# Forming both signs of a head pair's kv sum in one pass over the values, in a linear-attention block on one core

## The chip, the cores and the metric

The kernel runs on one core of a Trainium2 chip. The metric is the device time of one execution in microseconds. "Span" is the length of one profiled execution, which lies about 2 us under the timed value. Engines are called by the profile's names: PE (TensorE matmuls), PEld (its weight loads), DVE (VectorE), ACT (ScalarE), POOL (GpSimd).

## The reference

```python
# S = 2048 tokens, D = 448, H = 16 heads of Dh = 28, F = 1792
def A(x, wqkv, w_phi, wo):                       # linear attention
    q, k, v = split_heads(x @ wqkv)
    pq, pk = q @ w_phi, k @ w_phi                # per head
    phi_q = concat(softmax(pq), softmax(-pq))    # 56 features: two signs of 28
    phi_k = concat(softmax(pk), softmax(-pk))
    kv, z = sum_s phi_k[s] v[s]^T, sum_s phi_k[s]
    o = (phi_q @ kv) / (phi_q @ z + 1e-6)
    return merge_heads(o) @ wo
h   = x + A(layernorm(x), ...)
out = h + (sigmoid(g) * u) @ w_down              # g, u = layernorm(h) @ w_gate, w_up
```

The sums over tokens are a barrier: the first `num` product (`phi_q @ kv`, called num0) needs the kv sum of all 16 token blocks.

## The kernel before

Each engine works through a hand-made list of named operations (`ORDER`); semaphores between the lists come from the reads and writes that each operation declares. TensorE runs with its array split into two halves of 64 rows, LO and HI, whose matmuls are interleaved. The code keeps the two halves from writing one PSUM bank at the same time: an operation that puts the *other* half on a bank first waits for the previous one to be done with it. The code calls this crossing. A projection of one token block is two such operations, `pva` then `pvb`, on the same two banks with the halves exchanged; the list puts other work between them.

For each block t: ScalarE makes exp(+) and exp(-) of the projected keys (`ek`), VectorE sums them per head and sign (`ss`) and inverts (`rs`), POOL or VectorE multiplies (`phi`), and PE adds phi^T v into banks 6 and 7 (`kva`, `kvb`).

```python
NX, NO, NH, NPHI, NS, NE, NV, NSG, NHH = 3, 4, 3, 3, 3, 5, 5, 4, 2   # ring depths: NPHI phi slots, NV value slots
...
def kvf(first):                       # one kv op: 4 matmuls on LO, 4 on HI
    def f(e):
        def part(half, sg):           # weights: one sign of FOUR heads (120 columns); stream: their 4 x 29 values
            vv = v1[half, sv, :, :].rearrange("p (a h) e -> p a h e", a=2)
            return [(bk(6 + sg)[:GR, gg*4*EV:(gg+1)*4*EV], phi[half, sp, sg, gg, 0:GR],
                     vv[:, :, 2*gg:2*gg+2, :], ...) for gg in range(G)]
        sg = int(first != (t % 2 == 0))
        return both(e, part(LO, sg), part(HI, 1 - sg))
...
def kvmask():                         # keep each head's own block, 2 ops of 464 columns on VectorE
    for sg in (1, 0):
        op("dve", "kvz%d" % sg, lambda e, sg=sg: e.tensor_tensor(kvz[:, sg, ...], bk(6 + sg)[:GR, 0:G*4*EV]...,
           maskK[:]..., ALU.mult), r=[B(6 + sg), "maskK"], w=["kvz%d" % sg])
```

The softmax here doesn't subtract the row's maximum and nothing guards it: scores larger than these inputs give would overflow.

Of the kernel before, what the change touches and what calls it, by code (L numbers as in the profile page):

```python
# [6 lines left out]
ALU = mybir.AluOpType  # L7
# [11 lines left out]
class Graph:  # L19
# [86 lines left out]
    def emit(self, nc):  # L106
# [71 lines left out]
P = 128  # L178
D = 448
# [19 lines left out]

QL, QH = slice(0, 56), slice(64, GR)  # L200
# [3 lines left out]
        "x1 x0 ld_k0 x2 ld_k2 x4 x6 ld_v0 x10 ld_v2 ld_q2 x8 ld_q3 ld_q1 ld_q0 xT4 xT5 xT6 x14 x12 xT7 ld_woe1 xT8 "  # L204
        "xT9 xT10 xT11 xT12 xT13 xT14 ld_woo1 xT15 ld_wd0 ld_woe0 ld_wu2 ld_wg0 ld_wg2 ld_wd1 ld_wg3 ld_wu3 ld_woo0 "
        "ld_wu0 ld_wg1 ld_wd4 ld_wd6 ld_wu1 oT3 oT2 oT4 oT5 oT6 oT7 hT2 ld_wd3 ld_wd2 hT3 ld_wd5 hT4 oT8 oT9 hT5 hT6 "
# [4 lines left out]
        "wphi3 wphi2 wphi1 wphi0 wTe1 wTe0 wTe3 w2e0_0 w2e0_1 w2e0_2 w2e0_3 xn3 xn4 ek0 ek1 xn5 v1_0 v1_1 xn6 ek2 ek3 "  # L211
        "v1_2 w2e1_1 v1_3 xn7 ek4 w2e1_3 xn9 w2e1_2 ek5 v1_5 v1_6 ek6 xn11 ek7 xn12 ek8 v1_8 xn13 ek9 xn14 ek10 v1_10 "
        "ek11 v1_11 ek12 v1_12 ek13 v1_13 ek14 eq0_0 ek15 v1_14 v1_15 eq0_1 eq1_0 eq1_1 eq2_0 oT0e eq2_1 sq0 sq1 "
        "eq3_0 eq3_1 sig0_1 sig0_0 sig0_3 sig0_2 sig0_5 sig0_4 sig0_7 sq2 sig0_6 sq3 sig0_9 sig0_8 sig0_10 sig0_11 "
        "sq5 sig0_12 sig0_13 sq4 sq7 sig2_0 sig2_1 sq6 sig2_3 sig2_2 sig2_5 sig2_4 sig2_6 sig2_7 sig2_8 sig2_9 "
        "sig2_10 sig2_11 sig2_12 sig2_13 sig4_1 sq9 sig4_0 sig4_3 sq8 sig4_2 sig4_5 sig4_4 sig4_7 sig4_6 sig4_9 sq10 "
        "sig4_8 sq11 sig4_11 sig4_10 sig4_13 sig4_12 sig8_1 sig8_0 sq13 sig8_2 sig8_3 sig8_4 sig8_5 sq12 sig8_6 sq14 "
        "sq15 sig8_7 sig8_9 sig8_8 sig8_10 sig8_11 sig8_13 sig8_12 sig12_0 sig12_1 sig12_3 sig12_2 sig12_5 sig12_4 "
        "sig12_7 sig12_6 sig12_8 sig12_9 sig12_11 sig12_10 sig12_12 sig12_13 "
    ),  # L220
    "pe": (
        "warm0 wT1 wT0 warm1 xT1 warm2 xT0 warm3 wT2 wT3 w2m0_0 warm4 w2m0_1 w2m0_3 w2m0_2 warm5 xT2 warm6 ppa0 warm7 "
        "ppb0 xT3 vva0 vvb0 ppa2 ppb2 vva2 vvb2 kva0 w2m1_1 w2m1_0 kvb0 kva1 pva4 kvb1 pvb4 w2m1_3 w2m1_2 pva5 pva6 "
        "pvb5 pvb6 kva2 pqa0_0 kvb2 pva7 kva3 pvb7 pva8 kvb3 pvb8 pva9 kva4 pvb9 kvb4 pva10 kva5 pvb10 pva11 kvb5 "
        "kva6 pvb11 kvb6 pva12 kva7 pvb12 pva13 kvb7 pvb13 kva8 pva14 kvb8 kva9 pvb14 kvb9 pqb0_0 kva10 pva15 kvb10 "
        "kva11 pvb15 kvb11 kva12 pqa0_1 kvb12 kva13 pqb0_1 kvb13 kva14 pqa1_0 kvb14 kva15 kvb15 pqb1_0 pqa1_1 num0 "
        "num1 pqb1_1 pqa2_0 pqb2_0 num2 pqa2_1 oT0 pqb2_1 oT1 num3 woa0 wob0 pqa3_0 num4 pqb3_0 pqa3_1 pqb3_1 num5 "
        "hT0 hT1 ga0_1 gb0_1 ga0_0 num6 gb0_0 ga0_3 woa2 gb0_3 ga0_2 wob2 gb0_2 num7 ga0_5 gb0_5 ga0_4 gb0_4 ga0_7 "
        "gb0_7 ga0_6 num8 gb0_6 woa4 ga0_9 ga0_8 gb0_9 gb0_8 wob4 ga0_11 ga0_10 gb0_11 gb0_10 woa6 num9 wob6 ga0_13 "
        "ga0_12 gb0_13 gb0_12 dn0_0 dn0_4 ga2_0 ga2_1 gb2_0 gb2_1 dn0_8 dn0_11 ga2_3 num10 ga2_2 gb2_3 dp0_0 gb2_2 "  # L230
        "dp0_4 ga2_5 ga2_4 gb2_5 gb2_4 dp0_8 dp0_11 ga2_6 ga2_7 gb2_6 gb2_7 woa8 ga2_8 ga2_9 gb2_8 gb2_9 wob8 num11 "
        "ga2_10 ga2_11 gb2_10 gb2_11 dn2_0 ga2_12 ga2_13 gb2_12 gb2_13 dn2_4 dn2_8 ga4_1 num12 gb4_1 ga4_0 dn2_11 "
        "gb4_0 dp2_0 ga4_3 ga4_2 gb4_3 dp2_4 num13 gb4_2 ga4_5 dp2_8 gb4_5 ga4_4 dp2_11 gb4_4 ga4_7 num14 gb4_7 ga4_6 "
        "woa10 gb4_6 ga4_9 wob10 gb4_9 ga4_8 num15 gb4_8 ga4_11 woa12 gb4_11 ga4_10 wob12 gb4_10 ga4_13 dn4_0 ga4_12 "
        "gb4_13 gb4_12 dn4_4 ga8_1 ga8_0 gb8_1 gb8_0 dn4_8 dn4_11 ga8_3 ga8_2 dp4_0 gb8_2 dp4_4 dp4_8 gb8_3 ga8_4 "
        "dp4_11 gb8_4 ga8_5 woa14 gb8_5 ga8_6 wob14 gb8_6 ga8_7 dn6_0 gb8_7 dn6_4 ga8_8 ga8_9 dn6_8 gb8_9 gb8_8 "
        "dn10_0 dn6_11 ga8_11 ga8_10 gb8_11 gb8_10 dp6_0 dp6_4 dp6_8 ga8_13 ga8_12 gb8_13 gb8_12 dp6_11 dn10_4 dn10_8 "
        "ga12_0 ga12_1 gb12_0 dn8_0 dn10_11 gb12_1 ga12_2 dp10_0 ga12_3 dn8_4 gb12_3 gb12_2 dp10_4 dn8_8 ga12_5 "
        "dn8_11 ga12_4 gb12_5 gb12_4 dp8_0 dp8_4 ga12_7 ga12_6 gb12_7 dp10_8 dp10_11 gb12_6 dp8_8 dp8_11 ga12_9 "
        "ga12_8 gb12_9 gb12_8 dm14_0 dm12_0 dm15_0 ga12_11 ga12_10 gb12_11 gb12_10 dm12_4 dm14_4 dm13_0 ga12_12 "  # L240
        "ga12_13 gb12_12 gb12_13 dm15_4 dm14_8 dm15_8 dm12_8 dm15_10 dm14_10 dm14_12 dm14_13 dm15_12 dm12_10 dm12_12 "
        "dm15_13 dm12_13 dm13_4 dm13_8 dm13_10 dm13_12 dm13_13 "
    ),
    "dve": (
        "zero bd0 bst1 agg1 bst0 agg0 ve1_0 nm1_0 nm1_1 xn1 bst2 bst3 agg2 agg3 ve1_3 xT0e wTe2 bst5 nm1_3 bst4 agg5 "
        "agg4 bst6 xT1e ve1_4 bst7 agg7 agg6 bst10 xT2e bst11 agg10 xT3e nm1_6 ss0 agg11 rs0 ss1 bst8 rs1 bst9 agg8 "
        "ss2 agg9 ss3 w2e1_0 rs3 rs2 v1_4 bst15 bst14 bst13 ss4 agg14 agg13 bst12 rs4 agg15 agg12 xn10 ss5 ss6 v1_7 "
        "rs6 rs5 ss7 rs7 ss8 v1_9 ss9 rs9 rs8 xn15 ss10 ss11 rs11 rs10 ss12 rs12 ss13 phi11 ss14 rs13 rs14 phi13 ss15 "
        "rs15 phi15 kvz1 kvz0 rsm0 qq0 rsm1 b0 c0 qq1 den0 b1 rden0 c1 rsm2 den1 qq2 rden1 b2 c2 den2 oT1e rsm3 rden2 "
        "qq3 b3 c3 h0 den3 nm0 rden3 h1 rsm4 nm1 qq4 b4 c4 den4 hn0 hn1 rsm5 hT0e hT1e qq5 b5 c5 den5 rden4 hh0_1 "  # L250
        "rsm6 qq6 rden5 b6 hh0_0 c6 den6 rden6 hh0_3 h2 rsm7 hh0_2 qq7 b7 hh0_5 c7 nm2 hh0_4 den7 rden7 h3 nm3 rsm8 "
        "hh0_7 hh0_6 hn2 qq8 b8 hn3 hh0_9 hh0_8 h5 h4 nm5 c8 nm4 den8 hh0_10 hh0_11 rsm9 qq9 h6 h7 b9 c9 hh0_12 "
        "hh0_13 nm7 rden8 nm6 den9 hh2_0 hh2_1 hn4 rsm10 rden9 qq10 b10 hh2_3 c10 hh2_2 hn6 hn7 den10 hh2_5 hh2_4 "
        "fin0 fin1 hh2_6 hh2_7 hn5 rden10 hh2_8 hh2_9 h8 h9 hh2_10 hh2_11 rsm11 qq11 nm9 b11 hh2_13 c11 hh2_12 den11 "
        "rsm12 qq12 nm8 b12 c12 rden11 hh4_1 hh4_0 o10 den12 hh4_3 rsm13 qq13 b13 rden12 hh4_2 c13 hh4_5 den13 fin3 "
        "hn9 rden13 hh4_4 hn8 fin2 rsm14 hh4_7 o13 qq14 b14 c14 hh4_6 den14 h10 h11 nm10 hh4_9 nm11 rsm15 hn10 hh4_8 "
        "hn11 hh4_11 qq15 h13 h12 hh4_10 b15 c15 hh4_13 nm13 hh4_12 den15 nm12 rden15 o15 rden14 hh8_1 hh8_0 o14 "
        "hh8_2 hh8_3 fin4 fin5 hh8_4 hh8_5 h15 h14 nm14 hh8_6 nm15 hn12 hn14 hh8_7 hh8_9 hh8_8 hn13 hn15 hh8_11 "
        "hh8_10 hh8_12 hh8_13 fin6 fin7 hh12_0 hh12_1 hh12_3 hh12_2 hh12_5 hh12_4 hh12_7 fin11 hh12_6 fin9 fin10 fin8 "
        "hh12_8 hh12_9 hh12_11 hh12_10 hh12_12 hh12_13 fin14 fin15 fin12 fin13 "  # L260
    ),
    "pool": (
        "ident0 phipad wqpad mask0 neghalf ident ve1_1 pow1_1 pow1_0 xn0 v1ones mask1 nm1_2 ve1_2 pow1_2 nb1_2 xn2 "
        "pow1_3 nm1_4 nb1_3 pow1_4 nb1_4 ve1_6 opad0 mask2 pow1_6 nb1_6 phi0 phi1 nm1_8 ve1_8 pow1_8 nb1_8 xn8 phi2 "
        "phi3 ve1_12 nm1_12 pow1_12 kvzones nb1_12 phi4 phi5 phi6 phi7 phi8 phi9 phi10 phi12 phi14 o0 o1 o2 o3 ve0 "
        "pow2_0 ve1 pow2_1 o4 o5 o6 o7 ve2 pow2_2 ve3 pow2_3 ve5 ve4 pow2_4 o8 pow2_5 ve7 o9 ve6 pow2_7 pow2_6 ve8 "
        "ve9 o11 pow2_9 o12 pow2_8 ve10 pow2_10 ve11 pow2_11 ve12 pow2_12 ve14 pow2_14 ve15 ve13 pow2_15 pow2_13 "
# [38 lines left out]
def build(nc, A_x, A_wqkv, A_w_phi, A_wo, B_w_gate, B_w_up, B_w_down, out):  # L306
# [10 lines left out]
    with ExitStack() as es:  # L317
# [6 lines left out]
        maskK = sb("maskK", [GR, 4, EV], f32)  # L324
# [26 lines left out]
        wu_sb = sb("wu_sb", [P, KT, F])  # L351
        wd_sb = sb("wd_sb", [P, FT, D])
        xnT = [sb("xnT%d" % c, [P, KT, 512]) for c in range(NCH)]
        hnT = xnT
        eq = [sb("eq%d" % c, [GR, 2, G, 512]) for c in range(NCH)]
        hhT = [sb("hhT%d" % c, [P, FT, 512]) for c in range(NHH)]
        ek = hhT[1][:].rearrange("p f n -> p (f n)")[:, 0:NE * 2 * D].rearrange("p (s a d) -> p s a d", s=NE, a=2)
        ss = sb("ss", [P, NE, 2 * H], f32)
        rs = sb("rs", [P, NE, 2 * H], f32)
        phi = sb("phi", [P, NPHI, 2, G, P])  # L360
        v1 = sb("v1", [P, NV, H, EV])
        kvz = sb("kvz", [GR, 2, G, 4 * E])
        rsm = sb("rsm", [P, NS, H], f32)
# [524 lines left out]
```

## Time and profile before

| | before |
|---|---|
| time, median of 3 | 208.84 us (208.36 to 208.96) |
| first kv op / num0 / first gate matmul start | 17.56 / 47.58 / 61.09 us |
| the stage between the first two, here "kv stage" | 30.02 us |
| all 32 kv ops, each from its start to the next operation's start | 7.54 us |

Busy sums of matmuls overlap, so what a kv op costs PE is read from the timeline as the distance between starts (sums of these are good to about 0.03 us). Two more are needed: the end of the kv stage on PE and on VectorE (columns: start, time, engine, line, operation, count).

```profile
45.13 1.10 PE L289 MATMUL psum<-v,phi 64*120 64x116 bf16 x24
46.07 1.68 PE L289 MATMUL psum<-xnT,Wq 64*120 64x512 bf16 x14
47.58 0.60 PE L289 MATMUL psum<-kvz,eq 56*128 56x60 bf16 x31
```
```profile
46.27 1.19 DVE L657 TENSOR_TENSOR kvz<-psum,maskK 120x464 bf16<-120x464 f32 x2 [1.01 <-PE psum L289]
```

While VectorE copies the finished sum through the mask, PE runs two halves of the query projection. Num0 starts right behind them: the copy is hidden.

### The profile page before, as it was taken

The page shows a single profiled execution, that of the slowest core. Times are in us where ns is not written, and L with a number is a line of the kernel's source. Part 1 is how long each engine was busy: PE and PEld are TensorE (multiplying, and loading weights), DVE is VectorE, ACT ScalarE, POOL GpSimd, SP SyncE. Part 2 cuts the span into 40 slices and gives each one's busy share as a digit, 9 for nine tenths or more (in the row PEclk, how much of TensorE's full clock was granted, in tenths as well). Part 3 has the DMA queues.
Part 4 walks back from the last instruction along what each step waited for, and adds up shares of the span by engine and source line. Part 5 has one row for each costly group of instructions (what it writes and reads, how often), then busy time and mean ns, then how long its engine had stood idle before and what let it go on. Part 6 is the DMA issues. An engine that isn't in the chain of part 4 may idle for free.

```text
span 206.8 us, 5794 instructions
## 1 busy us (share of the span) xinstructions
PE 199.2 (96%) x2457; PEld 112.6 (54%) x2457; DVE 136.6 (66%) x343; ACT 95.2 (46%) x185; POOL 59.0 (29%) x99
## 2 busy tenths in 40 slices
PE   7999999999989999999999999999999999999991
PEld 2935666775446666777444444444555555544450
DVE  4899999978899897767768967446332513353151
ACT  2689999878792536222333342324323122122100
POOL 4868999831345404400032020001400000000000
PEclk9999999999999999999999999999999999999997
DMA  5945344899122270413005411030321000020013
GB/s 156 292 107 135 82 95 88 247 382 258 56 51 54 44 166 32 79 25 55 3 0 91 109 29 25 15 41 22 78 49 25 3 0 3 0 89 3 0 37 119
DMA packets 32722, 16.25 MB, mean 79 GB/s; under 512 B 24952, under 2 KB 31800, under 8 KB 32696
## 3 DMA queue, kind: packets, MB, share of 16 engines
q1 hardware_dynamic: 32192, 15.86, 31.2%
q8 instruction: 19, 0.31, 0.6%
q10 hardware_dynamic: 504, 0.03, 0.2%
q14 instruction: 7, 0.06, 0.1%
HBM read 8.34 MB, written 1.84 MB: 49 GB/s over the span
## 4 chain that ended last, share of the span: by engine, by line
PE 86%; DVE 4%; POOL 3%; DMA 2%; issue 1%; ACT 1%; SPq 1%
PE psum L289 79%; PE psum L814 5%; DMA x_sb<-in_A_x_dram 2%; POOL o_pad L700 1%; PE psum L478 1%; POOL rst L728 1%; SPq L388 1%; DVE hn_pad L732 1%; DVE st L485 1%; ACT eq L637 0%; PE psum L553 0%; ACT eq L638 0%; POOL xn_pad L514 0%; PE psum L464 0%; DVE hhT L788 0%
## 5 line engine op out<-in xcount | busy, mean ns | idle before, releaser
L289 PE MATMUL psum<-xnT,wg_sb 64*128 64x512 bf16 (+1 forms) x490 | 94.6, 333 | 0.7 <-DVE qq L685 0.6
L289 PE MATMUL psum<-xnT,wu_sb 64*128 64x512 bf16 (+1 forms) x490 | 94.5, 334 | 0.3
L787 ACT ACTIVATE sg_sb<-psum 128x512 bf16<-128x512 f32 (+1 forms) x70 | 35.0, 512 | 89.9 <-PE psum L289 89.4
L788 DVE SCALAR_TENSOR_TENSOR hhT<-sg_sb,psum 128x512 bf16<-128x512 bf16 (+1 forms) x70 | 39.1, 576 | 50.8 <-ACT sg_sb L787 50.3
L289 PEld LDWEIGHTS psum<-xnT,wg_sb 64*128 64x128 bf16 x490 | 43.8, 94 | 23.7 <-DVE hhT L788 4.8
L289 PEld LDWEIGHTS psum<-xnT,wu_sb 64*128 64x128 bf16 x490 | 43.9, 94 | 15.1 <-PE psum L289 1.4
L289 PE MATMUL psum<-wd_sb,hhT 64*128 64x448 bf16 x336 | 37.2, 349 | 0.0
L289 PEld LDWEIGHTS psum<-wd_sb,hhT 64*128 64x128 bf16 x336 | 17.3, 94 | 14.8 <-DVE x_sb L718 0.6
L607 POOL TENSOR_TENSOR phi<-hhT,rs 128x896 bf16<-128x896 bf16 x13 | 22.7, 1770 | 2.6 <-DVE rs L604 1.5
L289 PE MATMUL psum<-wv_sb,xnT 64*128 64x448 bf16 x112 | 22.0, 350 | 0.1
L289 PE MATMUL psum<-Wk,xnT 64*128 64x448 bf16 x112 | 22.0, 350 | 0.1
L726 POOL TENSOR_SCALAR ve<-ssq 128x1 f32<-128x1 f32 x16 | 3.1, 192 | 61.2 <-ACT junk L723 60.4
L603 DVE TENSOR_REDUCE ss<-hhT 128x32 f32<-128x896 bf16 x16 | 17.0, 1070 | 1.2 <-ACT hhT L600 1.1
L700 POOL TENSOR_TENSOR o_pad<-c_sb,rden 128x448 bf16<-128x448 bf16 x12 | 11.2, 937 | 19.0 <-DVE rden L695 17.4
L289 PE MATMUL psum<-xnT,Wq 64*120 64x512 bf16 x112 | 14.7, 381 | 0.2
L289 PE MATMUL psum<-wo_e,oT 64*128 64x448 bf16 x56 | 13.2, 350 | 0.2 <-DVE oT L471 0.2
L289 PE MATMUL psum<-wo_o,oT 64*128 64x448 bf16 x56 | 13.2, 350 | 0.1
L289 PEld LDWEIGHTS psum<-v,phi 64*120 64x120 bf16 x256 | 10.9, 131 | 3.3 <-PE psum L289 0.2
L821 DVE SCALAR_TENSOR_TENSOR x_sb<-psum,x_sb 128x448 bf16<-128x448 f32 x16 | 9.4, 619 | 3.5 <-PE psum L814 3.1
L723 ACT ACTIVATE junk<-x_sb,nm 128x448 bf16<-128x448 bf16 x16 | 10.6, 663 | 2.2 <-DVE nm L721 2.1
L289 PE MATMUL psum<-v,phi 64*120 64x116 bf16 x256 | 11.1, 213 | 0.1
L814 PE MATMUL psum<-wd_sb,hhT 128*128 128x448 bf16 x56 | 11.1, 353 | 0.0
(82 smaller groups left out, 240.2 us busy)
## 6 DMA issues: line engine op xcount, KB each, us to landing
out_dram<-x_sb SPq DMA_DIRECT2D x16, 112.0 KB, 1.8
x_sb<-in_A_x_dram SPq DMA_DIRECT2D x7, 224.0 KB, 4.3
wd_sb<-in_B_w_down_dram SPq DMA_DIRECT2D x7, 224.0 KB, 4.1
wg_sb<-in_B_w_gate_dram SPq DMA_DIRECT2D x3, 448.0 KB, 6.6
wu_sb<-in_B_w_up_dram SPq DMA_DIRECT2D x3, 448.0 KB, 9.9
wv_sb<-in_A_wqkv_dram SPq DMA_DIRECT2D x2, 224.0 KB, 4.8
wk_sb<-in_A_wqkv_dram SPq DMA_DIRECT2D x2, 196.0 KB, 3.9
wo_e<-in_A_wo_dram SPq DMA_DIRECT2D x1, 336.0 KB, 3.4
```

The costliest lines, as they stand in the source:

```text
L289: p = e.matmul(o, lhsT=w, rhs=r, start=st, stop=sp, tile_position=(row, 0))
L388: return op(eng, name, lambda e: e.dma_start(dst, src), r=r, w=w, dma="in" if eng == "sp" else "ain", nring=48 if eng == "sp" else 8, kb=kb)
L478: p = e.transpose(ps[:, kt * P:(kt + 1) * P], src, ident[:])
L603: op("dve", "ss%d" % t, lambda e: e.tensor_reduce(ss[:, s, :], eks, AX.X, ALU.add), r=[("ek", s)], w=[("ss", s)])
L607: return e.tensor_tensor(phi[:, sp, :, :, :].rearrange("p a g (f n) -> p (a g f) n", f=2)[:, :, 0:56].rearrange("p b (h d) -> p b h d", h= ...
L700: return e.tensor_tensor(o_pad[:, so, off:off + D].rearrange("p (h d) -> p h d", h=H), c_sb[:, s, :, 0:DH], rden[:, s, :][:, :, None].to_b ...
L723: op("act", "sq%d" % t, lambda e: e.activation(junk[:, t % 2, :], h_sb[:, t, :], ACT.Square, bias=nm2[:, t:t + 1], accum_out=ssq2[:, t:t + ...
L726: op("pool", "ve%d" % t, lambda e: e.tensor_scalar(ve2[:, t:t + 1], ssq2[:, t:t + 1], 1.0 / D, EPS, op0=ALU.mult, op1=ALU.add), r=[("ssq2" ...
L787: op("act", "sig" + nm, lambda e: e.activation(sg_sb[:, k, 0:N], bk(bg)[:, 0:N], ACT.Tanh, scale=0.5), r=[B(bg)], w=[("sg", k)])
L788: op("dve", "hh" + nm, lambda e: e.scalar_tensor_tensor(out=hhT[(t0 // 4) % NHH][:, ff, ns], in0=sg_sb[:, k, 0:N], scalar=1.0, in1=bk(bu)[ ...
L814: p = e.matmul(bk(b)[:, 0:D], lhsT=hb[:, ff, TS(t)], rhs=wd_sb[:, ff, :], start=ff == 0, stop=ff == FT - 1)
L821: op("dve", "fin%d" % t, lambda e: e.scalar_tensor_tensor(out=h_sb[:, t, :], in0=bk(b)[:, 0:D], scalar=0.5, in1=h_sb[:, t, :], op0=ALU.mul ...
```

## The change

It makes both exps of a head pair neighbours in memory, so that one matmul has both signs of two heads as its 128 weights and streams the pair's 58 values once, instead of streaming four heads' 116 values against one sign. The count of matmuls stays 256. The sums then lie by row half in a way that needs a copy which moves rows between halves, in four pieces. All order lists were made anew around this.

```diff
-    phi = sb("phi", [P, NPHI, 2, G, P])
-    kvz = sb("kvz", [GR, 2, G, 4 * E])
+    phi = sb("phi", [P, NPHI, 8, 2, 64])
+    kvz = sb("kvz", [P, 3, G, 2 * E])
@@ kvf
-    def part(half, sg):
-        vv = v1[half, sv, :, :].rearrange("p (a h) e -> p a h e", a=2)
-        return [(bk(6 + sg)[:GR, gg*4*EV:...], phi[half, sp, sg, gg, 0:GR], vv[:, :, 2*gg:2*gg+2, :], ...)
+    def part(half, a):
+        return [(bk(6 + a)[:, gg*2*EV:...], phi[half, sp, a*G + gg, :, :]..., v1[half, sv, 2*(a*G+gg):2*(a*G+gg)+2, :]..., ...)
@@ kvmask
-    for sg in (1, 0): op("dve", "kvz%d" % sg, <120 x 464>)
+    for k, src, a, dst, i in (("A", LO, 0, LO, 0), ("B", HI, 0, LO, 2), ("C", LO, 1, HI, 2), ("D", HI, 1, HI, 1)):
+        op(("dve", "act"), "kvz" + k, (<64 x 232 tensor_tensor>, <two activations of 64 x 116>), ...)
@@ ORDER (cut)
 pe   -  ... kva8 pva14 kvb8 kva9 pvb14 ... kva14 pqa1_0 kvb14 kva15 kvb15 pqb1_0 pqa1_1 num0
      +  ... pva14 kvb9 kva10 pvb14 ... pqa1_0 kvb13 kva14 pqb1_0 kvb14 kva15 kvb15 pqa1_1 num0
 act  +  kvzB behind eq0_1; oT1e from VectorE
 dve  -  kvz1 kvz0 ... c3 h0 den3 nm0 rden3 h1      +  kvzA kvzD kvzC ... c3 den3 rden3 h0 nm0 h1
 pool -  13 of the 16 phi                           +  14 of the 16 phi
 sp   -  xT7 ld_woe1 ... xT14 ld_woo1 xT15          +  xT7 ... xT15, then all wo, gate, up and down weights; x12 earlier
```

## The prediction

> **What bounds the kernel now.** I read the page first, then the table of five-microsecond windows, the lines split by shape, the timeline of TensorE (PE) around a few key blocks, and the chain of waits. The page says PE is busy almost throughout, and names the group that the change touches:
>
> ```profile
> PE 199.2 (96%) x2457; PEld 112.6 (54%) x2457; DVE 136.6 (66%) x343; ACT 95.2 (46%) x185; POOL 59.0 (29%) x99
> L289 PEld LDWEIGHTS psum<-v,phi 64*120 64x120 bf16 x256 | 10.9, 131 | 3.3 <-PE psum L289 0.2
> L289 PE MATMUL psum<-v,phi 64*120 64x116 bf16 x256 | 11.1, 213 | 0.1
> ```
>
> The kv sum is 256 matmuls of 116 columns. The lines by shape hold a ready-made model of what it becomes: the num products have 128 weight columns and stream 60.
>
> ```profile
> L289 PEld LDWEIGHTS psum<-kvz,eq 56*128 56x128 bf16 x256 | 5.2, 93 | 2.9 <-DVE den L692 1.4 <-DVE kvz L657 0.2
> L289 PE MATMUL psum<-kvz,eq 56*128 56x60 bf16 x256 | 6.0, 187 | 0.0
> ```
>
> Busy sums overlap (two row halves run at once, the modelled end has a long tail), so cost must be read as start-to-start time. The windows show which engines could take over in the stage where kv runs, 17 to 46 us:
>
> ```profile
> 25.00:30.00 5.00, 5.00 (x84) 3.22 (x80) 4.97 (x9) 4.98 (x11) 4.88 (x7) 1.00 0.47 93
> ...
> 30.00:35.00 5.00, 5.00 (x86) 3.22 (x82) 4.61 (x8) 4.73 (x10) 5.00 (x4) 1.00 0.38 71
> 35.00:40.00 5.00, 5.00 (x88) 3.66 (x88) 4.84 (x8) 4.22 (x9) 4.46 (x4) 1.00 0.82 210
> 40.00:45.00 5.00, 5.00 (x100) 3.96 (x96) 4.66 (x7) 4.42 (x8) 3.40 (x2) 1.00 1.01 362
> ```
>
> After the span, the columns are PE, PEld, DVE, ACT, POOL. PE issues without a gap, but DVE, ACT and POOL are each at 84 to 100% too: the stage is balanced, and a faster PE soon meets a neighbour. PE's work does fill it: twelve projections of 7 pairs at 0.19 us (16 us), 32 kv ops at some 0.22 (7), five q-projection halves (3.9) make 27 of the 27.2 us from 18.9 to 46.1.
>
> Now PE's starts. First a projection half, one kv op (8 matmuls, 4 pairs), and the next half; then the same with two kv ops; then one num (8 pairs); then two wo halves with nothing between.
>
> ```profile
> 30.48 0.35 PE L289 MATMUL psum<-Wk,xnT 64*128 64x448 bf16 x1
> ...
> 30.67 0.38 PE L289 MATMUL psum<-v,phi 64*120 64x116 bf16 x8
> 30.90 0.36 PE L289 MATMUL psum<-wv_sb,xnT 64*128 64x448 bf16 x1
> ...
> 32.24 0.60 PE L289 MATMUL psum<-v,phi 64*120 64x116 bf16 x16
> 32.67 0.35 PE L289 MATMUL psum<-wv_sb,xnT 64*128 64x448 bf16 x1
> ...
> 54.57 0.77 PE L289 MATMUL psum<-wo_o,oT 64*128 64x448 bf16 x2
> 54.99 0.36 PE L289 MATMUL psum<-wo_e,oT 64*128 64x448 bf16 x1
> ...
> 56.55 0.39 PE L289 MATMUL psum<-kvz,eq 56*128 56x60 bf16 x16
> 56.78 2.62 PE L289 MATMUL psum<-xnT,Wq 64*120 64x512 bf16 x20
> ```
>
> One kv op takes 0.43/2 = 0.215 us, 54 ns a pair. One num takes 0.23 us for eight pairs, 28 ns a pair. Between the wo halves PE stands: the last pair starts at 54.57 and streams 0.19, to 54.76, and the next half, which puts the other rows on the same banks, starts at 54.99. So a half that crosses banks needs **0.23 us of other work** in front of it. A kv op of 0.22 has been just that filler.
>
> From 73.6 us on PE has no gap to the end but the last output; its work there does not change. So a gain must be made before, and it carries through one to one.
>
> **What the Trainium skill says.** "TensorE: Matmul & The Clock Gate", § "Wait — 56ns, not 53.3ns?": warm starts are N/2.4 + 2.5 ns apart and never under about 25 ns. That is 50.8 for 116 columns and 26.7 for 58; the trace agrees (54, and 28 at 60 columns). So halving the stream still pays, but only just: it lands on the floor. The same page, § "Weight-path perf modes": fast weight load comes on when there are 128 weights. The trace agrees: 131 ns at 120 columns, 93 at 128; kv changes to 128. "TensorEngine Tiling (Array Packing)", § "Gotcha 1: PSUM Pressure": different row tiles cannot use one PSUM bank at once and software must keep them apart, which is the wait measured above as 0.23 us. "SBUF — State Buffer", § "Who interferes with whom": a DVE op with two SBUF inputs contends with POOL's reads. The trace agrees: the phi product on POOL takes 1.67 us a piece in a run of seven (11.69 us), but 2.31 and 1.97 us while DVE makes a phi beside it.
>
> **The change, part by part.**
> *The kv sum.* Before, each group of four heads streams its 116 values against one sign at a time: 2 signs x 4 groups x 2 halves x 16 blocks = 256. After, both signs of a head pair are the 128 weights and the pair's 58 values stream once: 8 x 2 x 16 = 256 again. Same count, half the stream. An op falls from 0.215 to 4 x 28 ns = 0.11 us: 32 x 0.105 = **3.4 us** off PE.
> *What the fillers give back.* I went through PE's new order for bank-crossing halves with just one kv op between: pva4, 5, 6, 9, 10 and 15 and pqa0_1, seven. There PE still waits 0.23 in all, so 7 x (0.23 - 0.11) = **0.8 us** is lost. The others now have two kv ops (0.22) between, which the order was evidently rebuilt for.
> *The masked copy.* Before: two DVE ops of 464 columns, 1.19 us, and num0 starts 1.51 us after the last kv (46.07 to 47.58), covered by 1.5 us of q-projection. After: four ops of 64 x 232, three on DVE, one on ACT as two of 116. From DVE's hhT rows (684 ns at 512 columns, 414 at 256: about 1.05 ns a column) one is 0.39 us, 0.31 apart: 1.0 us for three. With 0.2 us from kv's end to DVE's start and 0.1 to num0 that is 1.3 us, and only pqa1_1 (0.87) is left to cover it: **0.4 us** of PE idle, as pqb1_0 was moved ahead of the last kv.
> *Exps and phi.* Same elements, same instruction count; the exp writes runs of 56 instead of 448, and value copies with runs of 28 cost only 563 against 539 ns, so nothing.
> *Neighbours from the first ss to kvz.* DVE loses two statistics (1.1), a weight copy (0.5), one phi (1.0) and small things and gains one xn and one value copy (0.9): about -1.8. ACT loses one xn and one value copy and gains one weight copy: -0.75. POOL gains one phi: +1.7. POOL from phi0 near 15.8 needs 14 x 1.67 + 2.5 = 26 us, so phi14 by 41.8; PE will ask for it near 42.8. They fit, by about a microsecond each.
> *Start.* x and k are issued in the same order, the exps wait for the same four evacuations; ACT takes xT0 and xT1, DVE does all statistics of blocks 4 to 11 before its first ss. I expect +-0.3 us.
> *Weights behind the transposes.* wo is wanted near 52 us and gate weights near 59; about fifteen issues at 0.5 to 0.6 us from 33 us on still land in time. The queue has no share in the chain now: nothing.
> *After num0.* The chain from num0 to the first gate matmul lasts 13.5 us and does not depend on kv. One piece of it:
>
> ```profile
> 56.59 0.20 DVE rden L695
> ...
> 56.86 0.94 POOL o_pad L700
> ...
> 57.88 0.20 POOL ve L726
> ```
>
> o3 sits in front of the norm's ve0 on POOL because rden3 came after h0. The new DVE order makes rden3 first, so ve0 waits only for its square sum, ready at 57.4: **0.4 us** gained. oT1 copied on ACT and o7 on DVE I count as even.
> *Sum:* 3.4 - 0.8 - 0.4 + 0.4 = 2.6 us, less about 0.2 that I choose for slips between engines this full: 208.84 - 2.4 = **206.4 us**, 1.1% faster.
>
> **Rivals.** (1) *PE's whole 3.4 us and the order's gains arrive*, with the start improved too: some 204.5 us. For it: the new order was built around the short op. Against: seven thin fillers and an exposed masked copy. (2) *POOL or DVE becomes the bound*: fourteen phis on POOL, with ss0 perhaps 0.8 us later behind the statistics. Each phi slipping into a DVE phi's shadow costs 0.3 to 0.6 us. The gain falls under 1 us: about 208. (3) *Weights land late*: they share queue and engines with the transposes, and DMA reached 362 GB/s at 40 to 45 us. If wo or gate weights came after 52 or 59 us, PE would stop there and the time could rise to 209 or more. Moving them back a few microseconds of a slack near ten makes it unlikely.
>
> **Range and chances.** The size per kv op is well founded; the give-back of 1.2 us and the neighbours each carry some half a microsecond either way, the start and the stage of 47 to 73 us as much. I say 205.0 to 207.9 us eight times in ten. Over 2% faster means under 204.7, which needs rival 1 complete: 0.12. Over 2% slower needs rival 3: 0.02. Within 2%: 0.86.
>
> **What would show it.** A kv op alone 0.11 us from start to start, 0.23 where one is the only filler; weight loads of 93 ns; num0 near 45.5 instead of 47.6; a PE gap of some 0.4 us before num0 with DVE's kvz as releaser; ve0 waiting for the square sum, not for o3; first gate matmul near 58.6 instead of 61.1. Wrong if kv ops stay near 0.2 us, if phi on POOL or a weight's DMA releases PE in the kv or gate stage, or if gaps from 61 to 73 us grow.

## The result, and the profile after

| | before | after |
|---|---|---|
| time, median | 208.60 us (4 runs) | 207.31 us (4 runs, 207.10 to 207.47) |
| ratio | | 0.9937, interval 0.9915 to 0.9959 |
| span of the profile | 206.8 | 205.4 |
| first kv op | 17.56 | 17.17 |
| kv stage | 30.02 | 28.83 |
| num0 to the first gate matmul | 13.51 | 13.37 |
| all 32 kv ops, start to start | 7.54 | 5.41 |

A ratio here is the mean time of one kernel's fast runs over that of the other's in the same rounds, so it is not quite the ratio of the medians quoted. The change gains 0.6%, about 1.3 us: within 2%, as forecast, but 1.1 us less than the 2.4 us forecast (the time itself lies 0.9 us above the forecast 206.4).

The page's first line and the groups by shape, after:

```profile
PE 196.1 (96%) x2456; PEld 108.7 (53%) x2456; DVE 135.8 (66%) x341; ACT 96.2 (47%) x189; POOL 60.4 (29%) x101
...
L292 PE MATMUL psum<-v,phi 64*128 64x58 bf16 x256 | 7.8, 187 | 0.1
L292 PEld LDWEIGHTS psum<-v,phi 64*128 64x128 bf16 x256 | 7.0, 94 | 4.4 <-POOL phi L616 0.2 <-PE psum L292 0.2
```

The stream is half as long and the weight load fell from 131 to 94 ns, as the prediction wanted. New in the last column is a wait of weight loads for phi from POOL. It is one wait of 0.22 us, at the first kv op (17.11 us), so it says nothing yet of the course of the stage.

PE's starts in the kv stage, after. Two kv ops of 8 matmuls, one at 27.34 and one at 28.15:

```profile
27.34 0.29 PE L292 MATMUL psum<-v,phi 64*128 64x58 bf16 x8
27.58 0.36 PE L292 MATMUL psum<-wv_sb,xnT 64*128 64x448 bf16 x1
...
28.15 0.28 PE L292 MATMUL psum<-v,phi 64*128 64x58 bf16 x8
28.27 0.35 PE L292 MATMUL psum<-Wk,xnT 64*128 64x448 bf16 x1
```

The same op takes 0.24 us in the first place and 0.12 in the second. In the first it lies alone between `pva9` and `pvb9`, which cross; in the second between `pvb9` and `pva10`, which do not. The short op's saving is there only where PE had no other wait to fill.

The end of the kv stage, after, on PE and in the chain of waits (columns of the latter: start, time, what):

```profile
43.83 0.79 PE L292 MATMUL psum<-v,phi 64*128 64x58 bf16 x24
44.45 1.05 PE L292 MATMUL psum<-xnT,Wq 64*120 64x512 bf16 x8
46.00 0.63 PE L292 MATMUL psum<-kvz,eq 56*128 56x60 bf16 x32 [0.49 <-DVE kvz L677]
```
```profile
44.66 0.39 DVE kvz L677
45.05 0.01 issue
45.06 0.40 DVE kvz L677
45.47 0.03 issue
45.50 0.41 DVE kvz L677
```

Now PE waits for the copy. The query half between takes 0.87 us when nothing holds it up, so of the 1.55 us from 44.45 to 46.00 some 0.68 are lost. Three pieces of 64 x 232 follow each other without overlap: 1.24 us, no less than the two larger ones took before (1.19).

### The profile page after: what moved, and what is told of

The parts are those of the page before. It is cut to its first block, busy times and chain, and to the rows that moved or that the text cites. A ratio compares the mean times of both kernels' runs of the same rounds, so it can differ in the third digit from the quotient of the medians.

```text
span 205.4 us, 5793 instructions
## 1 busy us (share of the span) xinstructions
PE 196.1 (96%) x2456; PEld 108.7 (53%) x2456; DVE 135.8 (66%) x341; ACT 96.2 (47%) x189; POOL 60.4 (29%) x101
## 4 chain that ended last, share of the span: by engine, by line
PE 88%; DVE 7%; DMA 1%; issue 1%; ACT 0%; POOL 0%; DVEq 0%
PE psum L292 82%; PE psum L836 5%; DVE st L493 2%; DMA x_sb<-in_A_x_dram 1%; PE psum L561 1%; DVE b_sb L709 1%; DVE c_sb L712 1%; PE psum L486 1%; DVE kvz L677 1%; DVE x_sb L740 1%; DVE xnT L479 0%; DVE mv L494 0%; DVE hn_pad L754 0%; DVE x_sb L843 0%; DVE rsm L706 0%
## 5 line engine op out<-in xcount | busy, mean ns | idle before, releaser
L616 POOL TENSOR_TENSOR phi<-hhT,rs 128x896 bf16<-128x896 bf16 x14 | 24.0, 1735 | 0.9 <-PE psum L292 0.8
L722 POOL TENSOR_TENSOR o_pad<-c_sb,rden 128x448 bf16<-128x448 bf16 x11 | 10.3, 936 | 14.6 <-DVE rden L717 12.7
L292 PEld LDWEIGHTS psum<-Wk,xnT 64*128 64x128 bf16 x112 | 7.6, 94 | 5.4 <-ACT hhT L609 0.7
L493 DVE BATCH_NORM_STATS2 st<-x_sb 128x6 f32<-128x448 bf16 x16 | 9.3, 609 | 1.6 <-DMA x_sb<-in_A_x_dram 1.5
```

The source lines that it names most:

```text
L292: p = e.matmul(o, lhsT=w, rhs=r, start=st, stop=sp, tile_position=(row, 0))
L493: op("dve", "bst%d" % t, lambda e: e.bn_stats(st1[:, t, :], x_sb[:, t, :]), r=[("x", t)], w=[("st1", t)])
L616: return e.tensor_tensor(phi[:, sp, :, :, :].rearrange("p b a n -> p (b a) n")[:, :, 0:56].rearrange("p b (h d) -> p b h d", h=2), eks.rea ...
L722: return e.tensor_tensor(o_pad[:, so, off:off + D].rearrange("p (h d) -> p h d", h=H), c_sb[:, s, :, 0:DH], rden[:, s, :][:, :, None].to_b ...
```

## The experiments

Twelve kernels ran in three jobs of four, each job on one chip with the kernel before beside it: 208.50 us in the first, 208.53 in the second, 208.32 in the third. The last three columns are read from each run's profile. The order lists are printed differently in most of these kernels, which shifts their line numbers by a few.

| run | time, us | ratio to before | first kv op | kv stage | num0 to gate |
|---|---|---|---|---|---|
| before | 208.50 | | 17.56 | 30.02 | 13.51 |
| e1_sum_old_order | 208.18 | 0.9996 | 17.47 | 29.41 | 13.49 |
| e2_order_old_sum | 208.77 | 1.0016 | 17.07 | 30.56 | 13.35 |
| e3_paired | 208.06 | 0.9977 | 17.66 | 29.34 | 13.37 |
| e4_sp_old | 212.36 | 1.0183 | 17.35 | 34.03 | 13.37 |
| c_after | 207.25 | 0.9940 | 17.16 | 28.83 | 13.37 |
| e5_copy_dve | 207.82 | 0.9972 | 17.46 | 29.29 | 13.36 |
| e6_act_light | 207.09 | 0.9938 | 17.28 | 28.72 | 13.37 |
| e7_phi_light | 206.85 | 0.9928 | 17.05 | 28.59 | 13.37 |
| e8_wo_among | 207.40 | 0.9960 | 17.02 | 28.84 | 13.37 |
| e9_paired_act_light | 207.55 | 0.9972 | 17.09 | 29.24 | 13.36 |
| e11_copy_split | 207.59 | 0.9967 | 17.17 | 28.73 | 13.91 |
| e12_h0_first | 207.76 | 0.9973 | 17.51 | 28.81 | 13.62 |

Intervals of these ratios are 0.0013 to 0.0018 to either side (0.0027 for the first). How to read the table: the start of the first kv op moves by up to 0.6 us among kernels whose code up to there is the same, so a claim about a later stage is taken from that stage's own length, which repeats to about 0.01 us (28.83, 28.83, 28.84 in three profiles). C_after, the control, is the changed kernel itself:

> Control: the changed kernel itself once more, on the chip of the following three. Expected 207.1 to 207.6 us, ratio to the kernel before 0.992 to 0.996, num0 near 46.0 us and 1.4 us after the last kv op's end.

It came out at 207.25 us and 0.9940, with the stages of the first profile to within 0.01 us. In the third job, e8 stands for the changed kernel, which was not run there: its stages are the same, and its ratio there is 0.9960.

**The two halves of the change.** Does the new sum pay alone, and do the new orders?

```diff
 e1: the new sum, phi layout and masked copy, with every order list (and the warm-up matmuls) of before
     dve: kvz1 kvz0 -> kvzA kvzD kvzC;  act: + kvzB
 e2: every order list (and the warm-up matmuls) of after, with the old sum and copy
     dve: kvzA kvzD kvzC -> kvz1 kvz0;  act: - kvzB
```

> The new kv sum and masked copy, but every engine's queue in the order of the kernel before (the masked copy's four pieces in the place of the two old ones). If TensorE alone bounds the kv stage, the old order should do as well: it also has seven places where one kv op is the only filler between two halves that cross banks (0.8 us given back), but 1.5 us of q-projection still covers the masked copy; then 3.4 - 0.8 = 2.5 us come off and the time is 206.1 to 206.4 us. If instead DVE, ACT or POOL become the bound at once, so that the new order is what lets the shorter stream show, it is 207.6 to 208.4 us, with phi on POOL or exps on ACT as releaser in the kv stage.

> The new queue orders with the old kv sum and the old two-piece masked copy. If the gain comes from the shorter stream, this is no faster than before: the start is some 0.4 us earlier (first kv near 17.2 us), but the masked copy is covered by only 0.9 us of work instead of 1.5, so 208.3 to 208.9 us. If the reordering itself carries the gain, it is near the changed kernel, 207.2 to 207.7 us.

Neither gains: 0.9996 and 1.0016, against 0.9937 and 0.9940 for both together. So the gain is an interaction, and the profiles say of what. In the kv stage, whose length repeats better than the times, e1 is 0.61 us shorter than before and e2 0.54 us longer, yet both together are 1.19 us shorter. In e1 the kv ops need 0.84 us less, but PE then stands for phi (the timeline of PE in e1):

```profile
41.24 0.29 PE L293 MATMUL psum<-v,phi 64*128 64x58 bf16 x8 [0.45 <-POOL phi L617]
...
43.74 0.29 PE L293 MATMUL psum<-v,phi 64*128 64x58 bf16 x8 [0.29 <-POOL phi L617]
```

With the old lists PE asked for phi as fast as POOL made it, and a faster PE meets POOL: the prediction's second rival, for the old orders. This is read from the trace; no run gave e1 a lighter POOL. In e2 the new orders cost 0.54 us in the kv stage, above all because they leave one query half where two had hidden the copy (the timeline of PE in e2):

```profile
47.63 0.56 PE L292 MATMUL psum<-kvz,eq 56*128 56x60 bf16 x28 [0.42 <-DVE kvz L660]
```

From e2 to after, the lists being the same, the new sum brings 1.73 us in the kv stage, 2.06 of it in the kv ops (7.47 to 5.41). From before to e1 it brought 0.61.

**Single fillers.** The prediction counts seven places where one kv op alone fills a crossing. Can pairs of them fill better?

```diff
 e3, pe list, five places such as
-pvb8 kvb3 pva9 kva4 pvb9 kvb4 pva10 kva5 pvb10
+pvb8 pva9 kvb3 kva4 pvb9 pva10 kvb4 kva5 pvb10
```

> The changed kernel with TensorE's order alone altered so that two kv ops instead of one stand between the halves that cross banks in five more places (pva6, pva9, pva10, pva15, pqa0_1). If a half that crosses banks needs 0.23 us of other work ahead of it, each place gives 0.11 us back: first num product 0.3 to 0.5 us earlier than in the changed kernel (46.0 us), time 206.8 to 207.0 us. If POOL's phi products set the pace by now, TensorE only waits for them instead: 207.2 to 207.4 us, unchanged.

It is slower, which neither side of the expectation had. The kv ops fall to 4.53 us, by 0.88, but the stage grows by 0.51: the projections, from start to start, take 1.40 us more. I first read the waits in its profile as waits for ScalarE to empty the banks, and tested that:

```diff
 e6: after, with the second exp of blocks 5 to 15 on half its columns (a wrong result on purpose; it stayed within the comparison's tolerance)
-    return e.activation(ek[:, s, :, 1, :], src, ACT.Exp, scale=-1.0)
+    n = 8 if t < NE else 4
+    return e.activation(ek[:, s, 0:n, 1, :], src[:, 0:n, :], ACT.Exp, scale=-1.0)
 e9: the same edit on e3
```

> Wrong result on purpose: from block 5 on, the exp of the negated keys runs over half its columns (224 of 448), which takes some 0.19 us per block, 2 us in all, off ScalarE in the kv stage and touches nothing else. Theory (ScalarE, at 100% in 25 to 35 us, holds PE's banks and so paces the stage): num0 0.5 to 1.0 us earlier after kva0 than in the control, time 0.5 to 1.0 us less. Rival (POOL's phi, or PE's own order with single kv fillers, paces it): num0 within 0.2 us of the control.

> Wrong result on purpose: the paired order (two kv ops as filler in five more places, which alone took 29.34 us from kva0 to num0 against 28.83 of the changed kernel) with the lighter second exp of blocks 5 to 15 (which alone took 28.72). Theory (a single kv op between two bank-crossing halves ran in a wait that ScalarE's evacuation of the banks would else have filled, so the forecast give-back of the fillers was only there with a lighter ScalarE): kva0 to num0 28.0 to 28.5 us, ratio to before 0.989 to 0.993. Rival (the paired order loses for another reason, such as POOL's phi): 29.0 us or more, ratio above 0.996.

In both the theory missed. With ScalarE's exps relieved the changed kernel gains 0.11 us in the stage, and the paired one 0.10 (29.34 to 29.24). ScalarE is at 100% from 25 to 35 us, yet its exps are not what sets the length. The timelines of PE and of DVE in e9 show another wait:

```profile
27.80 0.84 PE L294 MATMUL psum<-Wk,xnT 64*128 64x448 bf16 x2
28.30 0.36 PE L294 MATMUL psum<-wv_sb,xnT 64*128 64x448 bf16 x1
```
```profile
27.57 0.63 DVE L481 CAST v<-psum 128x448 bf16<-128x448 f32 x1 [0.34 <-PE psum L294]
28.11 1.08 DVE L615 TENSOR_REDUCE ss<-hhT 128x32 f32<-128x896 bf16 x1
```

`pva10` starts 0.50 us after the last pair of `pvb9` instead of 0.19. It needs the bank that VectorE's copy of block 8's values empties, and that copy stood idle until 27.57, for PE. By the code it writes the value slot that kv op `kvb3` reads (five slots: block 8 follows block 3), and this list put `kvb3` later, at 27.17 with `kva4`. So a kv op is also what frees a slot, and moving it can cost elsewhere what it saves. This was read from the trace; a run with a sixth slot was not made. The same happens once more at 30.18 us, but it is not the whole loss: e9's weight loads also wait 1.4 us, in four places, for ScalarE's value copies (0.4 us in two places in the changed kernel), and the pair of kv ops at 42.79 us takes 0.69 us, waiting for POOL's phi. How the loss divides among these stays open.

**POOL.**

```diff
 e7: after, with the phi product of blocks 3 to 15 on 12 of its 16 pieces (a wrong result on purpose; two of these blocks, 10 and 15, are VectorE's)
-    ...[:, :, 0:56], eks..., rs...to_broadcast([P, 16, 2, DH])
+    n = 16 if t < NPHI else 12
+    ...[:, 0:n, 0:56], eks...[:, 0:n], rs...[:, 0:n]...to_broadcast([P, n, 2, DH])
```

> Wrong result on purpose: from block 3 on, the phi product runs over 12 of its 16 pieces, a quarter less, some 0.4 us per block on POOL and nothing else touched. Theory (ScalarE paces the stage): num0 within 0.3 us of the control, only the two PE waits for phi near 38 and 43 us (0.39 and 0.43) vanish. Rival (POOL paces it): num0 0.8 us or more earlier and the time 0.8 us or more less.

The stage shrinks by 0.24 us and the ratio goes from 0.9940 to 0.9928 in the same job: neither zero nor 0.8. It is mostly one place: the pair of kv ops at 42.72 took 0.43 us in the changed kernel, and here (the timeline of PE in e7)

```profile
42.59 0.39 PE L292 MATMUL psum<-v,phi 64*128 64x58 bf16 x16
42.82 0.86 PE L292 MATMUL psum<-xnT,Wq 64*120 64x512 bf16 x6
```

takes 0.23. The other wait, 0.39 us at 37.85, stayed at 0.39; e6 shortened it to 0.31, so that one hangs on ScalarE at least in part. So neither ScalarE nor POOL, relieved alone by this much, gives back more than a quarter of a microsecond. Both at once were not tried, and no run relieved VectorE; the view of PE's waits from 17 to 46 us in the changed kernel names VectorE for the masked copy alone. That the rest is PE's own order is likely, but not shown.

**The masked copy.** One run lengthens it on VectorE, one shortens it there.

```diff
 e5:  dve kvzA kvzD kvzC        -> kvzA kvzD kvzC kvzB      act: - kvzB
 e11: dve kvzD (64 x 232)       -> its first head only, 64 x 116
      act kvzB                  -> kvzB kvzE                kvzE: the other head of D, ordered behind kvzD
```

> The changed kernel with the fourth piece of the masked copy (kvzB) moved from ScalarE to VectorE, behind the other three; a fourth piece at the 0.41 us pace of the others. Theory (the masked copy is exposed before num0 and carries through one to one): num0 0.4 us later relative to the last kv op's end, time 0.3 to 0.5 us above the control. Rival (what follows num0 has slack that swallows it): num0 0.4 later but the first gate matmul and the end unchanged, within 0.15 us of the control.

> The changed kernel with half of one piece of the masked copy (kvzD, 64 x 116) moved from VectorE to ScalarE behind kvzB: VectorE 0.41 + 0.25 + 0.41 instead of 3 x 0.41, ScalarE 0.60 + 0.30. Theory (the copy's end sets num0 and carries through): num0 0.15 us earlier after the last kv op, time 0.1 to 0.2 us under the changed kernel, ratio to before 0.992 to 0.9945. Rival (ScalarE, whose exp of the queries comes 0.3 us later, then holds num0 or the q projections): no gain or a loss of up to 0.3 us.

E5: four pieces take 1.68 us instead of 1.24, the wait before num0 grows from 0.49 to 0.97, the kv stage by 0.46, and what follows num0 keeps its length (13.36). So the copy carries through one to one. The time rises by 0.57 us, of which the later start in its profile may be a part. E11 gains 0.10 in the stage and loses 0.54 behind it, where PE now waits for ScalarE's exp of the queries, pushed back by the extra piece (the timeline of PE in e11):

```profile
47.74 0.43 PE L294 MATMUL psum<-xnT,Wq 64*120 64x512 bf16 x2 [0.53 <-ACT eq L649]
```

The rival was right: three pieces on VectorE and one on ScalarE is the better division.

**After num0.** The prediction expects 0.4 us because the new list puts den3 and rden3 ahead of h0.

```diff
 e12, dve list
-den3 rden3 h0 nm0 h1
+h0 den3 nm0 rden3 h1
```

> The changed kernel with the kernel before's places of h0 and nm0 on VectorE: h0, den3, nm0, rden3, h1 instead of den3, rden3, h0, nm0, h1. Theory (putting den3 and rden3 ahead of h0 freed POOL's ve0 of o3 but made h0 0.45 us later, so the step came to 0.14 us and not 0.4): ve0 waits for o3 again and the first gate matmul starts 13.4 to 13.6 us after num0 (13.37 in the changed kernel), time within 0.2 us. Rival (den3 and rden3 simply stand in the way of h0): 13.1 us or less after num0 and the time 0.25 us or more less.

The stretch from num0 to the first gate matmul is 13.62 us with the old places, 13.37 with the new. POOL's view in e12 shows the old trouble again, o3 (`o_pad`) right in front of ve0:

```profile
55.72 0.94 POOL L724 TENSOR_TENSOR o_pad<-c_sb,rden 128x448 bf16<-128x448 bf16 x1 [2.48 <-DVE rden L719]
56.74 0.19 POOL L750 TENSOR_SCALAR ve<-ssq 128x1 f32<-128x1 f32 x1
```

And in the changed kernel:

```profile
54.62 0.94 POOL L722 TENSOR_TENSOR o_pad<-c_sb,rden 128x448 bf16<-128x448 bf16 x1 [1.70 <-DVE rden L717]
56.10 0.19 POOL L748 TENSOR_SCALAR ve<-ssq 128x1 f32<-128x1 f32 x1 [0.54 <-ACT junk L745]
```

So the move is worth 0.25 us by itself (the time, 0.4 us above e8's, missed the expected 0.2; e12 also started 0.5 us later). POOL was freed by more, but ve0 now waits 0.54 us for the square sum of h0, because den3 and rden3 push h0 back: h0 starts 8.46 us after num0, against 8.31 in e12 and 8.19 in the kernel before.

**The transfers.**

```diff
 e4: sp list of before, whole
 e8: sp list of after, with only these two moved back
-xT7 xT8 ... xT14 xT15 ...
+xT7 ld_woe1 xT8 ... xT14 ld_woo1 xT15 ...
```

> The changed kernel with only the DMA queue's order put back to that of before (two small wo loads among the x transposes again, x8 and x12 later). If queueing the weights behind the transposes plays no part, as predicted, 207.1 to 207.5 us. If it is a part of the gain (transposes landing earlier), 207.7 us or more.

> The changed kernel with only the two wo loads (woe1, woo1) put back among the x transposes, behind xT7 and xT14, as the kernel before had them; every x load keeps its new place. Theory (the place of the weights plays no part; the 5 us that the run with the whole old DMA order lost came from the late x loads of blocks 12 and 14): within 0.2 us of the changed kernel, ratio to the kernel before 0.992 to 0.996. Rival (the transposes were waited for behind the weights): 0.3 us or more slower, with a PE or ScalarE wait on an xT load in the kv stage.

E4 is 1.8% slower than before, for a reason that has nothing to do with weights. The old list loads x12 at 17.68 us instead of 10.17, and the new VectorE list asks for that block's statistics early (the waits of DVE in e4, with columns total, times, longest, and the timeline of PE):

```profile
DVE st L495 <- DMA x_sb<-in_A_x_dram: 6.2, 3, 4.5
```
```profile
26.13 0.37 PE L294 MATMUL psum<-v,phi 64*128 64x58 bf16 x8 [3.72 <-POOL phi L618]
```

The stand costs more than its 3.72 us: the granted clock is 0.50 from 26 to 29 us and 0.80 from 29 to 30, and PE's work from 26.13 to 31.03 us takes 4.90 us where the changed kernel needs 3.51 (22.04 to 25.55), which need not all be the clock's doing. E4 therefore did not test the weights; e8 does. That the late x12 is the cause is read from e4's trace; no run moved x12 alone. With the two wo loads among the transposes every stage has the length it had, and PE's waits name no transfer. Its timed ratio of 0.9960 lies 0.002 above the control's on another chip, with overlapping intervals; the traces show no stage to which that could belong. No version beat the changed kernel: e6 and e7, the only lower times, leave out work.

## Why the prediction was right or wrong

*Right: the class, the range, and the mechanism of the kv ops and of the exposed copy.* The median of 207.31 us lies within 205.0 to 207.9, but the gain is 1.3 us where 2.4 were forecast. What the prediction listed as signs was there: kv ops of 0.12 alone and 0.23 to 0.24 as a lone filler, weight loads of 94 ns, a gap before num0 with VectorE's kvz as releaser, ve0 waiting for the square sum. Num0 came at 46.00 (forecast near 45.5), the first gate matmul at 59.37 (near 58.6). Two of its signs of being wrong were there as well, both small: phi on POOL releases PE twice in the kv stage (0.22 us at 17.11, 0.15 at 43.02), and a gap between 61 and 73 us grew (0.61 us at 72.04, against 0.12 at the same matmul before).

*"The kv sum", 3.4 us, and "What the fillers give back", 0.8: right in size.* The seven places were exactly the seven of 0.23 to 0.24 us (starts 18.76, 20.34, 22.04, 27.34, 29.02, 38.99, 40.67).

*The 0.2 us "for slips between engines this full": too small.* The kv ops save 2.13 us, not 3.4 - 0.8 = 2.6. The waits are in four other places: 0.22 us at 26.36 and 0.15 at 21.14 instead of 0.12, and 0.39 at 37.85 and 0.43 at 42.72 instead of 0.23 for a pair, together about 0.5 us. E7 shows that the last is POOL's; e6 shortens the first to 0.14 and the third to 0.31, so ScalarE has a share. "They fit, by about a microsecond each" failed for POOL by that microsecond: its last phi ended at 42.97, not 41.8, and was wanted near 42.8. POOL's sum left out two waits of 0.40 and 0.41 us, before the phis at 33.80 and 35.91, in which POOL stood until PE had freed a phi slot, so the orders of the two engines hold each other up. Another 0.26 us of the stage, outside kv ops and copy, was not traced further.

*"The masked copy", 0.4 us: mis-sized, it is 0.68.* The step that failed is "0.31 apart". The pieces started 0.40 and 0.44 us apart and did not overlap, so three took 1.24 us instead of 1.0. E5 shows that this counts one to one. Such an overlap was there in the kernel before, where two pieces of 0.64 us took 1.19; a likely reason why it is gone is in the last section.

*"After num0", 0.4 us: mis-sized, it is 0.14.* E12 puts the den3 and rden3 step at 0.25; the prediction took POOL's gain and left out that the same move delays h0. What offsets the remaining 0.11 was not isolated.

*"Start", taken as 0 +-0.3: 0.4 us gained in the profiles.* Of eleven profiles with the new lists and a first kv op read, eight lie between 17.02 and 17.28, but three between 17.46 and 17.66, as late as the old lists' 17.47 and 17.56. So it is a gain in most executions, not in all, and for the forecast it was luck.

*"Weights behind the transposes", nothing: right,* by e8.

*From the first gate matmul on, taken as unchanged: 0.3 us lost,* 0.19 of it up to 72.04 us, where a new wait of 0.61 us for VectorE's hhT shows in profiles with the new lists. The cause stays open: e1, with the old lists and without that wait, loses the same 0.3 us there (146.0 us to the end, against 145.7 before and 146.0 after).

*"Exps and phi", nothing: nearly.* ScalarE's exps took 571 and 575 ns instead of 554, some 0.6 us over the 32 of them, and VectorE's two phis 1.41 us each instead of 1.09; neither was isolated.

*Slips in the working that change nothing:* the 27 us of PE's work from 18.9 us on count 32 kv ops where 29 lie there (6.7 us), and leave out 0.5 us of the query weights' product; and "84 to 100%" does not hold for POOL from 40 to 45 us (3.40 of 5.00).

*Sum, in the profiles:* start +0.39, kv ops +2.13, copy -0.68, rest of the kv stage -0.26, after num0 +0.14, gate stage and later about -0.3: 1.4 us, the difference of the spans. The forecast of 2.4 is missed by three small terms (copy, slips and the rest of the kv stage, after num0), partly made good by the start. And rival 2 was nearer than its argument allowed: e1 shows it complete when the orders stay as they were.

## What to carry to other kernels

In a stage where all engines are full, making one operation shorter pays only together with a new order: alone, the short sum gave 0.61 us in its stage and nothing that the times resolve, and the new order gave nothing. Before counting the saving of a shorter operation, ask what each instance was good for besides its result: here seven were the only filler of a bank change, some covered a wait for another engine, and some freed a ring slot that a later copy wanted. And when an operation is moved ahead to clear one wait, look at what it is put in front of.

## What the Trainium skill lacked or had wrong

- "VectorE: DVE Perf Modes", § "Two Vector instructions with no wait between them", gives a model in which an instruction whose input or output starts in another quadrant than the last one's is held until all earlier Vector instructions have finished. I left it out of the prediction. The copy's pieces, which exchange row halves, agree with it: three pieces at starts 44.66, 45.06 and 45.50 with no overlap, 1.24 us, and four in 1.68; the kernel before's two pieces, which both read and write from row 0 on, overlap by 0.09 us (0.64 us each, together 1.19). The page lacks a figure for what a hold costs; no run here set pieces of one size with equal and with unequal quadrants, so the cause is not isolated.
- "TensorEngine Tiling (Array Packing)", § "Gotcha 1: PSUM Pressure", says that row tiles must be kept apart on a bank, but not what it costs. Here a lone filler of 0.12 us takes 0.23 to 0.24 from its start to the next half's.
- No page tells that shortening an operation which fills such a wait pays nothing there: 32 kv ops lost half their stream, and of 3.4 us only 2.13 were saved.
